# Linear attention beside a gated MLP on one core: the key-value sums come out turned, and q moves to groups of 128 and 64 columns

## The chip, the cores and the metric

The kernel runs on one core of one Trainium2 chip. A core has TensorE (matrix multiplication; it reads its operands from SBUF and writes its sums to PSUM), VectorE, ScalarE, GpSimd (POOL in the profile) and SyncE (SP, which here only issues DMAs). PSUM has eight banks of 128 partitions by 512 fp32 values. The metric is the device time of one launch in microseconds. Each kernel is run several times and the median counts. The profile comes from one further execution.

## The reference, cut to what matters

```python
xn = _layernorm(x)                                   # x: 2048 x 576
q, k, v = split(xn @ wqkv)                           # 32 heads of 18 columns
phi = lambda t: jnp.where(t > 0, t + 1, jnp.exp(t)) + 1e-6
pq, pk = phi(q), phi(k)
kv = jnp.einsum("bhsd,bhse->bhde", pk, v)            # one 18 x 18 matrix a head
z = jnp.einsum("bhsd->bhd", pk)
num = jnp.einsum("bhqd,bhde->bhqe", pq, kv)
den = jnp.einsum("bhqd,bhd->bhq", pq, z)[..., None] + 1e-6
s = (num / den).reshape(B, S, D) @ wo                # 2048 x 576
h = gelu(xn @ w_gate) * (xn @ w_up)                  # 2048 x 4608
return x + s * silu(h @ w_down)
```

There is no mask over time: kv and z are sums over all 2048 tokens, so no query can be finished before all keys and values are done.

## The kernel before, in words

Tokens are held in four blocks (tb = 0 to 3) of 512, and each block in four tiles of 128. The 576 columns of x are two halves of 288 = 128 + 128 + 32 rows of contraction. Precision is kept by splitting operands into a high and a low part in fp32r, a fast matmul type: a product is hi x hi + hi x lo + lo x hi. PASSES (line 40) lists seven such matmuls for a half of the contraction, in which the 32-row remainders share one; a product over both halves takes 14.

The program has these stages:

1. **Weights, normalization, k and v** (lines 917 to 998). w_tiles, load_w, load_w2, prep_hi and prep_lo bring the weights in and split them: ScalarE writes the high part, VectorE or POOL the low part. load_w2 loads both column halves of q for one half of the contraction into the slot b12; the second such load waits until POOL is done with the first. For each tile of tokens k_mm and v_mm make k and v, k_post applies phi, and v_post copies v into va, in groups of seven heads (126 columns; the last group has four heads, 72 columns) with a column of ones behind each group. kv_mm multiplies pk by va for each of the five groups and accumulates over all 16 tiles into two PSUM banks (kv_a, kv_b): rows are columns of k, columns are columns of v, and the column of ones gives z.
2. **q** (lines 1000 to 1023). q_mm makes one group of q for a block of 512 tokens, transposed: 14 matmuls with the weights of 126 or 72 columns as the stationary operand. Blocks 0 and 1 are stored to DRAM (q_store) and reloaded later (q_load); 2 and 3 stay in SBUF (q_hold, which can run a list of other work between its groups).
3. **kv times wo** (kv_done, kv_turn, kv_wo; lines 419 to 479). kv_done masks the sums to their heads' 18 x 18 blocks (kvm), and builds zc, which holds z by head. kv_turn transposes kvm on TensorE (kt) and ScalarE copies it to kvt. kv_wo multiplies it by wo in fp32, two matmuls a group (kw), and splits the results into kvh and kvl (kv4 for the last group). The output projection is thereby folded into the sums.
4. **den, scale, s** (lines 498 to 551), for blocks 2, 3, 0, 1 in this order. den multiplies zc by q in fp32 (d: five matmuls of 32 columns by 512 tokens), takes the reciprocal on VectorE and splits it into rd, high and low. scale spreads a head's reciprocal to its columns with the 0/1 matrix sel (b: two fp32r matmuls a group, high and low, with 32 rows), multiplies q by it and splits the product into pq. s_mm makes a tile of 128 tokens of s: 15 passes (5 groups by 3) for two column halves, 30 matmuls of 288 columns.
5. **Gated MLP**: the matrices of the gate and the up projection by a scheme of seven products for a 2 x 2 block multiplication (matrix, lines 627 to 666), then the down projection (down_all). The change does not touch this code.

In stage 1, and again from line 1063 on (`fixed[0] = True`), instructions that go through act, vec and mm keep the written order on their engines. From line 1000 to 1062 (`fixed[0] = False`) a planner orders them: each engine's queue is filled by priority in written order, and an instruction whose operands or buffers the planner expects late lets later ones pass. Once ordered, each engine works its queue strictly in order. SP issues DMAs in order, too, and holds at one that has to wait.

PSUM is given out by pools. Up to line 1015 the pool has two single banks and two pairs beside the two sum banks; `banks(4, 2)` (line 1018) opens one with four single banks and two pairs. A new pool waits until the old one has been emptied. SBUF slots named by big(i, ...) hold different tiles one after the other; b12 serves the raw q weights, then four operand copies, then wo, then sel and rd.

## Time and profile before

| what | us |
|---|---|
| median of 3 runs | 1565.93 |
| lowest and highest | 1565.88, 1567.93 |
| the profiled execution's own time | 1567.46 |
| its span | 1565.8 |
| TensorE busy | 1526.4 |
| VectorE, ScalarE, GpSimd busy | 1077.4, 550.1, 558.5 |
| first product of the gated MLP begins | 355.89 |

The profiled execution's own time includes what lies around the span. In the profile an operation's row names the line, the engine, the tile that it writes and those that it reads, and its shape: partitions by elements. A matmul's row says rows of contraction by stationary columns. PEld rows are loads of the stationary operand, which overlap with matmuls. An fp32 matmul shows as two records, an fp32r matmul as one. Matmuls are pipelined, so a record lasts longer than the distance to the next one's start. The chain of waits is followed back from the last instruction, at each step to what released it; its rows give a start, a length and a count.

### The profile page before, as it was taken

How to read it: one execution, taken by the hardware profiler on the slowest of the kernel's cores; microseconds unless marked ns; L12 is line 12 of the kernel's file. 1: busy time of each engine (PE TensorE's matmuls, PEld its weight loads, DVE VectorE, ACT ScalarE, POOL GpSimd, SP SyncE). 2: the span in 40 equal slices, each digit the busy share in tenths (PEclk: the TensorE clock that was granted, in tenths of full speed). 3: DMA queues.
4: the chain of work that ended last, by engine and by line, in shares of the span. 5: the costliest groups of instructions: out<-in, count | busy, mean ns of one | idle time of the engine just before them, and what ended most of it. 6: DMA issues, size and time to landing. Idle time of an engine off the chain costs nothing.

```text
span 1565.8 us, 22593 instructions
## 1 busy us (share of the span) xinstructions
PE 1526.4 (97%) x8569; PEld 1346.7 (86%) x8569; DVE 1077.4 (69%) x1565; ACT 550.1 (35%) x939; POOL 558.5 (36%) x513
## 2 busy tenths in 40 slices
PE   4999999999999999999999999999999999999998
PEld 4987995888888888888888888888889999999998
DVE  6668336544887787777787877778885565655775
ACT  3435214233322223222322232323234555444443
POOL 3143523022655544456555544565440020000220
PEclk9999999999999999999999999999999999999999
DMA  4326000444443433344434333344469757787873
GB/s 151 131 108 234 1 5 0 168 167 174 165 165 129 162 120 124 135 154 165 165 140 154 140 109 143 138 165 165 157 218 329 249 164 270 241 260 248 279 248 112
DMA packets 112287, 256.60 MB, mean 164 GB/s; under 512 B 10086, under 2 KB 38502, under 8 KB 110134
## 3 DMA queue, kind: packets, MB, share of 16 engines
q1 hardware_dynamic: 110114, 242.31, 43.7%
q0 software_dynamic: 2064, 12.85, 2.3%
q8 instruction: 67, 1.10, 0.3%
q14 instruction: 42, 0.34, 0.1%
HBM read 157.47 MB, written 97.65 MB: 163 GB/s over the span
## 4 chain that ended last, share of the span: by engine, by line
PE 91%; DVE 5%; ACT 2%; DMA 1%; issue 1%; POOL 0%; DVEq 0%; ACTq 0%; POOLq 0%
PE bd L827 25%; PE al L622 14%; PE ga L622 14%; PE de L622 14%; PE be L622 7%; PE s L539 4%; PE q L370 3%; PE pv L99 3%; PE pk L99 2%; PE d L501 1%; PE kv_a L99 1%; PE b L516 1%; PE xt L171 1%; DVE xo_B L96 1%; DVE x L96 1%
## 5 line engine op out<-in xcount | busy, mean ns | idle before, releaser
L827 PE MATMUL bd<-t,s 128*128 128x288 f32 x3024 | 401.5, 295 | 2.2 <-DVE u L96 2.2
L827 PEld LDWEIGHTS bd<-t,s 128*128 128x128 f32 x3024 | 400.9, 188 | 2.8 <-DVE u L96 2.7
L96 DVE TENSOR_TENSOR s<-sr,s 128x512 fp32r<-128x512 f32 x252 | 181.1, 760 | 119.7 <-ACT s L93 117.8
L93 ACT ACTIVATE s<-sr 128x512 fp32r<-128x512 f32 x252 | 149.0, 625 | 192.4 <-PE bd L827 128.4
L102 POOL TENSOR_TENSOR hs<-h,h 128x512 f32<-128x512 f32 x72 | 100.5, 1405 | 231.2 <-DVE h L96 228.4
L93 ACT ACTIVATE h<-h 128x512 f32<-128x512 f32 x108 | 67.1, 633 | 247.5 <-DVE h L96 132.1
L102 POOL TENSOR_TENSOR sx<-sx 128x288 f32<-128x288 f32 x24 | 27.9, 1183 | 318.6 <-DVE sx L96 317.6
L96 DVE TENSOR_TENSOR wa<-raw,wa 128x256 fp32r<-128x256 f32 x72 | 77.2, 1072 | 56.2 <-ACT wa L93 53.0
L102 POOL TENSOR_TENSOR sm<-raw 128x384 f32<-128x384 f32 x72 | 75.6, 1050 | 96.9 <-DMA raw<-in_wgu_dram 79.3
L96 DVE TENSOR_TENSOR h<-h,u 128x512 f32<-128x512 f32 x108 | 97.6, 904 | 3.7
L102 POOL TENSOR_TENSOR td<-td 128x288 f32<-128x288 f32 x72 | 71.5, 993 | 57.4 <-DMA td<-in_wd_dram 53.2
L93 ACT ACTIVATE wa<-sm 128x1152 fp32r<-128x1152 f32 x36 | 41.8, 1160 | 139.3 <-PE de L622 139.3
L96 DVE TENSOR_TENSOR wa<-sm,wa 128x768 fp32r<-128x768 f32 x72 | 63.7, 885 | 33.6 <-ACT wa L93 32.8
L96 DVE TENSOR_TENSOR wb<-sm,wb 128x256 fp32r<-128x256 f32 x72 | 60.8, 845 | 20.5 <-ACT wb L93 20.0
L96 DVE TENSOR_TENSOR wb<-raw,wb 128x256 fp32r<-128x256 f32 (+1 forms) x108 | 71.8, 664 | 1.7 <-ACT wb L93 0.2
L93 ACT ACTIVATE u<-al 128x512 f32<-128x512 f32 x72 | 40.9, 592 | 91.2 <-PE al L622 91.2
L370 PE MATMUL q<-xo_B,wq 128*126 128x512 f32 (+1 forms) x240 | 66.3, 407 | 0.0
L96 DVE TENSOR_TENSOR u<-u,ga 128x512 f32<-128x512 f32 x72 | 49.4, 686 | 22.7 <-PE ga L622 22.0
L622 PE MATMUL al<-xo_B,wa 128*128 128x512 f32 x252 | 63.1, 390 | 0.8 <-ACT s L546 0.8
L622 PE MATMUL ga<-xr_B,wb 128*128 128x512 f32 x252 | 63.0, 389 | 0.0
L622 PE MATMUL be<-xo_T,wa 128*128 128x512 f32 x252 | 63.0, 390 | 0.0
L622 PE MATMUL de<-xo_T,wb 128*128 128x512 f32 x252 | 63.0, 390 | 0.0
(163 smaller groups left out, 2992.3 us busy)
## 6 DMA issues: line engine op xcount, KB each, us to landing
sr<-hs SPq DMA_DIRECT2D x252, 256.0 KB
hs<-h SPq DMA_DIRECT2D x68, 512.0 KB
raw<-in_wgu_dram SPq DMA_DIRECT2D x36, 768.0 KB
hs<-hs SPq DMA_DIRECT2D x102, 256.0 KB
td<-in_wd_dram SPq DMA_DIRECT2D x18, 576.0 KB
td<-td SPq DMA_DIRECT2D x18, 576.0 KB
tr<-td SPq DMA_DIRECT2D x16, 576.0 KB
tr<-in_wd_dram SPq DMA_DIRECT2D x12, 576.0 KB
```

The lines of the kernel that those rows point to most:

```text
L93: pin(nc.scalar.activation(*args, **kw))
L96: pin(getattr(nc.vector, op)(*args, **kw))
L99: pin(nc.tensor.matmul(*args, **kw))
L102: tc.keep_in_program_order(getattr(nc.gpsimd, op)(*args))
L171: pin(nc.tensor.transpose(xts[n][:, j, c], xs[:, j, c], ident))
L370: nc.tensor.matmul(pq[0:wdt, :], w_part(0, j, wi, gi * GW, gi * GW + wdt, rows), xo[s][nm][0:rows, xi, :], start=(n == 0), stop=(n == 2 * ...
L501: nc.tensor.matmul(pd[0:H, :], at["zc"][0:wdt, gi, :], ph[tb][0:wdt, gi, :], start=(gi == 0), stop=(gi == NHG - 1),)
L516: nc.tensor.matmul(pb[0:wdt, :], at["sel"][:, gi, 0:wdt], at["rd"][:, i, :], start=(i == 0), stop=(i == 1),)
L539: nc.tensor.matmul(pss[:, c, 0:HALF], pqs[tb, gi][a][0:wdt, t * P : (t + 1) * P], kw[0:wdt, c * HALF : (c + 1) * HALF], start=(n == 0), st ...
L622: nc.tensor.matmul(o, w[0:rows, wi, :], xop[0:rows, xi, :], start=(start and n == 0), stop=(n == len(PASSES) - 1), skip_group_check=True,)
L827: nc.tensor.matmul(banks[j][:, 0:HALF], hw[n, s][:, a, t * P : (t + 1) * P], w[:, c, g % 4], start=(new and g == 0 and m == 0), stop=(g == ...
```

## The change

In kv_mm the operands swap: va is stationary and pk moves, so the sums come out as columns of v by columns of k, which is the form that kv_wo needs as its stationary operand. The ones move to the first column of va, so z is row 0 of each group. kv_turn is dropped. wo gets a zero row 0 and two more columns, of which one has a 1 in row 0: kv_wo thereby yields z as an extra column, from which zc is made.

q's groups become five of 128 columns. The last group had 72 columns; 64 of them stand twice in group 4 (rows 0 to 63 and 64 to 127), and the other eight are dealt out, two each, into rows 126 and 127 of groups 0 to 3. The host lays out the q weights so (wq, 640 columns, apart from wkv). In group 4, pq then holds the high part in rows 0 to 63 and the low part in rows 64 to 127, and kv4 holds the high part twice and, in a second tile, the low part with zeros below: two passes do what three did. The rows of kvh, kvl and zc for the eight dealt-out columns are brought to partitions 126 and 127 by twelve small DMAs on SP's queue.

den makes its block in two column halves, tokens 0 to 255 to PSUM rows 0 to 63 and tokens 256 to 511 to rows 64 to 127, each with z twice. VectorE then takes the reciprocal over 128 rows by 256 columns. rd holds high and low rows of both halves with zeros elsewhere, sel holds the 0/1 matrix four times, and scale needs one matmul of 128 rows.

In the order, kv_wo moves into the list of q_hold(2) behind the third group, ahead of the change of pools; make_sel follows; den(2) moves behind the first group of q_hold(3). The scratch of POOL-issued DMAs goes from 4096 to 2048 bytes.

```diff
 def load_w2 / prep_hi / prep_lo
-        raw = big(i, [P, 2, 3, HALF], F32, f"rw_{m}_{j}")
+        raw = big(i, [P, 2, 3, NC2[m]], F32, f"rw_{m}_{j}")
...
 def kv_mm
-                kv_out(gi)[0:wdt, 0 : wdt + 1],
-                pk[:, gi * GW : gi * GW + wdt], va[:, gi, 0 : wdt + 1],
+                kv_out(gi)[0 : wdt + 1, 0:wdt],
+                va[:, gi, 0 : wdt + 1], pk[:, gi * GW : gi * GW + wdt],
...
 def q_mm
-                    pq[0:wdt, :],
-                    w_part(0, j, wi, gi * GW, gi * GW + wdt, rows),
+                    pq, w_part(0, j, wi, gi * P, (gi + 1) * P, rows),
...
 def make_masks
+        nc.gpsimd.memset(mask[0:1, :], 1.0)
...
+        nc.gpsimd.memset(at["zc"][Q4:P], 0.0)
...
 def load_wo
+        at["wo"] = w = big(12, [P, 4, D + 2], F32, "wo_t")
+        at["wo4"] = w4 = tmp([P, D + 2], "wo4")
+        for t in (w, w4[:, None, :]):
+            nc.gpsimd.memset(t[0:1, :, 0:D], 0.0)
+            nc.gpsimd.memset(t[:, :, D:], 0.0)
+            nc.gpsimd.memset(t[0:1, :, D : D + 1], 1.0)
...
-    def kv_turn():
...
 def kv_wo
+        for gi in (4, 0, 1, 2, 3):
...
+            r, x_ = slice(0, Q4 if gi == 4 else GW), slice(Q4, W4)
+            z, src = pw[:, 1, HALF : HALF + 1], pw[:, :, 0:HALF]
+            if gi == 4:
+                nc.vector.tensor_copy(zx[x_], z[x_].to_broadcast([W4 - Q4, 2]))
+                parts(kv4[x_, 2, :], kv4[x_, 3, :], src[x_])
+                nc.scalar.activation(two(kv4[Q4:P, 0, :]), src[r], AF.Copy)
+
+            nc.vector.tensor_scalar(
+                zc[r, gi, :].rearrange("p (r h) -> p r h", r=2),
+                mh[r, gi, None, :].to_broadcast([r.stop, 2, H]), z[r], None, op0=ALU.mult,
             )
+            if gi == 4:
+                parts(kv4[r, 0, :], kv4[r, 1, :], src[r])
+            else:
+                parts(kvh[r, gi, :], kvl[r, gi, :], src[r])
+        for gi in range(4):
+            r, e = slice(Q4 + 2 * gi, Q4 + 2 * gi + 2), slice(GW, P)
+            nc.sync.dma_start(
+                out=zc[e, gi, :].rearrange("p (r h) -> p r h", r=2)[:, :, H - 1], in_=zx[r]
+            )
+            for t, i in ((kvh, 2), (kvl, 3)):
+                nc.sync.dma_start(out=t[e, gi, :].bitcast(F32), in_=kv4[r, i, :].bitcast(F32))
...
 def make_sel
+        for i in range(4):
+            r = slice(i * H, (i + 1) * H)
+            if i % 2:
+                nc.scalar.activation(sel[r], one, AF.Copy)
+            else:
+                nc.gpsimd.tensor_copy(sel[r], one)
...
 def den
+        for gi in range(NHG):
+            for i in range(2):
+                nc.tensor.matmul(
+                    pd[2 * H * i : 2 * H * (i + 1), 0:HB], at["zc"][:, gi, :],
+                    ph[tb][:, gi, i * HB : (i + 1) * HB],
+                    start=(gi == 0), stop=(gi == NHG - 1),
+                )
+        r = gl_tile([P, HB], f"r_{tb}")
...
+        for i in range(2):
+            c = slice(i * HB, (i + 1) * HB)
+            rows, low = slice(2 * H * i, 2 * H * (i + 1)), slice(H * (2 * i + 1), 2 * H * (i + 1))
+            nc.scalar.activation(rd[rows, c], r[rows], AF.Copy)
+            nc.vector.tensor_sub(rd[low, c], r[low], rd[low, c].bitcast(F32))
 def scale
-        for i in range(2):
-            nc.tensor.matmul(
-                pb[0:wdt, :], at["sel"][:, gi, 0:wdt], at["rd"][:, i, :],
-                start=(i == 0), stop=(i == 1),
-            )
+        nc.tensor.matmul(pb, at["sel"][:, gi, :], at["rd"], start=True, stop=True)
...
 def s_mm
+        steps = [
+            (pqs[tb, gi][a], kw[:, gi, :])
+            for gi in range(4) for a, kw in ((0, at["kvh"]), (0, at["kvl"]), (1, at["kvh"]))
+        ] + [(pqs[tb, 4][0], at["kv4"][:, i, :]) for i in range(2)]
...
-    q_hold(2, 7, [kv_done, kv_turn])
+    q_hold(2, 7, [kv_done, lambda: None, kv_wo])
+    make_sel()
     psum["stage"].close()
     stage.close()
     banks(4, 2)
-    kv_wo()
-    make_sel()
-    den(2)
     differences(1, nc.gpsimd)
-    q_hold(3, 8, [lambda: None, lambda: None, lambda: scale(2, 0),
+    q_hold(3, 8, [lambda: den(2), lambda: None, lambda: scale(2, 0),
                   lambda: (scale(2, 1), scale(2, 2)), lambda: (scale(2, 3), scale(2, 4))])
...
-        "TRN2", target_bir_lowering=False, num_devices=1, dynamic_dma_scratch_size=4096
+        "TRN2", target_bir_lowering=False, num_devices=1, dynamic_dma_scratch_size=2048
```

More of the change, by code (lines that the diff above doesn't have):

```diff
@@ L32 @@
 W4 = WIDTHS[4]
+Q4 = 64
+Q2 = NHG * P // 2
 LN_EPS = 1e-5
@@ new lines, in make_sel @@
+    def make_sel():
+        n = NHG * P
+        buf = big(12, [P, n + TBN], F32R, "aux")
+        at["sel"] = sel = buf[:, 0:n].rearrange("p (g j) -> p g j", g=NHG)
+        at["rd"] = rd = buf[:, n : n + TBN]
+        one = tmp([H, NHG, P], "self")
+        nc.gpsimd.memset(one, 1.0)
+        four, last = one[:, 0:4, 0:GW], one[:, 4, :].rearrange("p (r j) -> p r j", r=2)
+        for o, pattern, base in ((four, [[GW, 4], [1, GW]], 0), (last, [[0, 2], [1, Q4]], 4 * GW)):
+            nc.gpsimd.affine_select(
+                out=o, in_=o, compare_op=ALU.is_ge, fill=0.0, base=base,
+                pattern=pattern, channel_multiplier=-DH,
+            )
+            nc.gpsimd.affine_select(
+                out=o, in_=o, compare_op=ALU.is_ge, fill=0.0, base=DH - 1 - base,
+                pattern=[[-s_, n_] for s_, n_ in pattern], channel_multiplier=DH,
+            )
@@ L530, in s_mm @@
+        h = slot([P, 2, TBN], F32R, f"pq_{tb}_{gi}")
+        pqs[tb, gi] = [h[:, i, :] for i in range(2)]
+        split(h[:, 0, :], h[:, 1, :], p)
     def s_mm(tb, t):
```

200 lines of the change are left out of this document (86 added, 114 removed).

## The prediction

> **What bounds the kernel now.** I read the page first, then the chain of waits from 215 us to 360 us, because the diff touches work only up to there; the gated matrices and the down projection behind it (355.89 us to the end) keep their code.
>
> ```profile
> PE 1526.4 (97%) x8569; PEld 1346.7 (86%) x8569; DVE 1077.4 (69%) x1565; ACT 550.1 (35%) x939; POOL 558.5 (36%) x513
> PE 91%; DVE 5%; ACT 2%; DMA 1%; issue 1%; POOL 0%; DVEq 0%; ACTq 0%; POOLq 0%
> ```
>
> TensorE is busy 97% of the span and makes 91% of the chain that ended last. A TensorE instruction that goes away is therefore worth its issue spacing, unless another engine then ends the wait. The same chain by time, in the stage that the change rewrites:
>
> ```profile
> by line: PE s L539 45.7%; PE q L370 19.8%; PE d L501 12.4%; PE b L516 7.3%; PE kw L469 3.7%; PE pv L99 2.6%; PE al L622 2.4%; PE pk L99 1.7%; PE kv_a L99 1.2%; issue 1.2%; PE kt L451 0.5%; PE be L622 0.5%; ACT s L546 0.5%; ACT kvt L455 0.4%
> 225.15 0.45 PE kt L451 x4
> ...
> 226.32 0.26 PE kt L451
> ...
> 236.61 1.48 issue
> 238.09 2.18 PE kw L469 x8
> ...
> 311.94 2.51 PE b L516 x10
> 314.45 4.41 PE d L501 x10
> 318.87 16.12 PE s L539 x120
> 334.99 2.63 PE b L516 x10
> 337.62 17.50 PE s L539 x120
> ...
> 355.89 3.48 PE al L622 x14
> ```
>
> Columns are start, length, what, and how many instructions. The four token blocks run in the order 2, 3, 0, 1; the rows from 311.94 are the full period of block 0 (23.05 us to 334.99) and then block 1, which has no den behind it. Within a period TensorE goes from b to d to s with no gap. Of the 145 us, s has 45.7%, d 12.4% (18.0 us, 4.5 a block), b 7.3% (10.6 us).
>
> **The change, part by part.** *s, 14 passes for 15.* Each of 16 s_mm calls issues 28 matmuls of 288 columns where it issued 30. A full block takes 16.12 us for 120, so 0.134 us each; 32 go: -4.30 us. The columns copied into spare rows ride in matmuls that run anyway.
>
> *b, one spread matmul for two.* 40 become 20, at 2.51/10 = 0.25 us: 10.6 us becomes 5.3. The contraction grows from 32 to 128 rows, at the same 512 columns. Not all of the 5.3 is kept, because b also covers VectorE:
>
> ```profile
> 312.63 1.88 DVE L527 TENSOR_TENSOR ph<-ph,b 126x512 f32<-126x512 f32 x3 [10.01 <-PE b L516]
> 314.43 1.89 DVE L109 TENSOR_TENSOR pq<-ph,pq 126x512 fp32r<-126x512 f32 x3
> 319.62 3.34 DVE L507 RECIPROCAL r<-r 32x512 f32<-32x512 f32 x1
> 335.68 1.88 DVE L527 TENSOR_TENSOR ph<-ph,b 126x512 f32<-126x512 f32 x3 [8.05 <-PE b L516]
> 340.73 1.29 DVE L109 TENSOR_TENSOR pq<-ph,pq 126x512 fp32r<-126x512 f32 x2 [0.17 <-ACT pq L108]
> ```
>
> A multiply takes 0.63 us and frees one of the four single banks; five b in 1.25 us outrun it. The fifth b waits for the first multiply and den for the second, so den begins near 0.35 + 2 x 0.63 = 1.6 us instead of 1.25: 0.4 us goes back in blocks 3 and 0. VectorE needs from 335.68 to 342.02 (6.3 us) for block 1's multiplies and subtractions. s consumes a group each 0.8 us and can take the next tile's matmuls meanwhile, so I return 0.6 us in block 1. Net -3.9 us (ends -5.3 and -2.5).
>
> *Clock in block 1.* s takes 17.50 us there against 16.12 in block 0, with the same 120 matmuls.
>
> ```profile
> 336.00:339.00 3.00, 3.00 (x13) 2.23 (x12) 3.00 (x6) 1.84 (x3) 0.00 (x0) 0.71 0.81 262
> ```
>
> That is a stretch of 3 us: after its length come the busy times of the engines, and the third number from the end is the granted clock. It is 0.71, right behind 2.63 us of b on 32 rows. With half as many b, on 128 rows, I expect no dip: -1.4 us (ends -1.4 and 0).
>
> *kv_turn goes.* The sums come out turned, so five transposes and two copies leave the chain: 225.15 to 226.60, 1.45 us including the wait for ScalarE. Swapping operands in kv_mm keeps 80 fp32 matmuls, one column narrower: nothing.
>
> *den in halves.* Ten fp32 matmuls of 256 columns stand where five of 512 stood, the halves to PSUM rows 0-63 and 64-127.
>
> ```profile
> L501 PE MATMUL d<-ph,small x40: 589/592/617, 240.2 to 318.3; 126*32 126x512 f32 x32, 72*32 72x512 f32 x8
> ```
>
> One fp32 matmul shows as two records of 0.592 us, begun 0.441 us apart. In series the halves cost the same 4.4 us, and no gain is one end. The two halves share neither array columns nor PSUM rows, and if each pair runs side by side the block costs 2.2 us; with a start-up of 0.15 (0.592 - 0.441) I say 2.4. Over four blocks: -8.0 us (ends -8.8 and 0). No row shows two matmuls with disjoint columns. The nearest is that TensorE begins a record before its predecessor ends and loads weights under it (86% beside 97%), so it overlaps what shares nothing; I take the side-by-side end. VectorE's reciprocal drops from 3.34 to about 1.7 us (half the columns, four times the rows), which gives slack but is hidden. Two ScalarE copies and two subtractions for one each also fit, since s covers them.
>
> A weighing on den: the row says that d ends at 314.45 + 4.41 = 318.86 and s begins at 318.87, so leaving a 32-column matmul costs nothing visible. The Trainium skill ("TensorEngine Tiling (Array Packing)", section Key Properties) says that changing the tiling mode drains TensorE. By that rule eight edges at the 0.151 us by which records overlap would give back 1.2 us, and the sum would be 1549.8 for 1548.6 below; by the row it is nothing, and this case's trace speaks against it for this edge.
>
> *kv_wo earlier, with small transfers.* It moves from after the change of PSUM pools (236.61, the 1.48 us wait for the last q to be evacuated) to behind the third q group of block 2. Its ten matmuls (290 columns for 288) stay. Their waits for ScalarE and VectorE, filled by d before, are now filled by the fourth and fifth q.
>
> ```profile
> L108 ACT ACTIVATE kvh<-kw x4: 650/650/651, 239.3 to 243.4; 126x576 fp32r<-126x576 f32 x4
> L109 DVE TENSOR_TENSOR kvl<-kw,kvh x4: 757/757/758, 240.0 to 244.1; 126x576 fp32r<-126x576 f32 x4
> 1.26 0.90 SPq L248 DMA_DIRECT2D rw<-in_wqkv_dram  x2
> 0.81 2.98 DMA x<-in_xe_dram
> 236.26 0.61 POOL L487 MEMSET self<- 32x630 f32 x1
> ```
>
> Group 4 has three ScalarE copies and two subtractions, 3 x 0.65 + 0.76 = 2.7 us before its bank is free; 6.6 us of q lie beside that. The pool change still waits for the last q: 1.48 us as before. Twelve transfers then queue on SP at 0.45 us each (two issued in 0.90), and each lands at most 2.98 us after its issue (the row of a load of 384 KB). den(2), now behind the first q group of block 3, needs the first ten of them (the fourth den column is tenth): 4.5 + 2.98 = 7.5 us after group 4 is cut. Until then TensorE has two q groups (6.6), the other four kw (4.4), the pool change (1.48) and a q group (3.3), 15.8 us, less the 2.7 of the cut: 13 us of cover. If it is gone, den(2) holds TensorE. SP's next behind them is the reload of stored q, which waits for scale(2) anyway. POOL's selector work grows to some 4.4 us (one memset and two copies of that size, five selects of that size or smaller, two short memsets) and can hold back the last q addition that den(2) reads: +1.0 us (ends 0 and +3). The memsets ahead of the wo loads, and those in the masks, queue on POOL among its additions; POOL is busy 36% of the span, so 0. The POOL-issued reloads get half the descriptor space:
>
> ```profile
> xr_T<-kept_T POOLq DMA_DIRECT2D x4, 1280.0 KB, 8.6
> ```
>
> Each lands in 8.6 us, and the last two are issued behind scale(1) with four tiles of s (about 15 us) and two products (2 x 3.17) ahead of their first reader: 0, unless they queue.
>
> *Prep of the q weights.* 320 columns for 288, on a stretch of chain not set by TensorE:
>
> ```profile
> 87.83 0.82 ACT wq L93
> 88.71 0.81 POOL wq L272
> 89.53 2.29 POOL wq_l L272
> 91.89 0.80 POOL wq L272
> 92.72 4.41 DMA rw<-in_wqkv_dram
> 97.15 0.93 ACT wq L93
> ...
> 106.56 1.61 PE kv_a L99 x6
> ```
>
> The six steps sum to 10.06 us and 11% of that is 1.1 us. The 2.29 is a POOL operation held up by VectorE and a transfer has a fixed part, so I take +0.7 us (ends +0.4 and +1.1). q itself stays 14 matmuls a group:
>
> ```profile
> 127.48 3.28 PE q L370 x14
> 362.54 3.17 PE ga L622 x14
> ```
>
> q with 126 weight columns takes 3.28, a gate product with 128 takes 3.17. If 128 columns are the reason, 20 groups give 2.2 us. Both stream 512 columns 14 times, so I take the difference for something at a group's edge, and count 0 (ends -2.2 and 0). Phi, stores and reloads of 128 rows for 126 take the same free sizes: 0.
>
> The sum: -4.3 - 3.9 - 1.4 - 1.45 - 8.0 + 1.0 + 0.7 = -17.35 us. The profiled execution took 1567.46 us with a span of 1565.8; the median of the three runs is 1565.93, so the span stands for the median, and the forecast is **1548.6 us**. Ends taken together: 1540 to 1564.
>
> **The rivals.** *The halves run one after the other.* Then den keeps 4.4 us a block: 1548.6 + 8.0 = 1556.6 us. For it: every matmul in this trace begins only when its predecessor has streamed, and den's record pairs too. Against it: only that they share nothing. The Trainium skill ("TensorE: Matmul & The Clock Gate", Part 3) states that matmuls on separate column groups run at once, 2.38 times faster for three of 32 columns; no run here shows it yet, and that rule is for my forecast.
>
> *The planner's new order loses cover.* From 108 us on the engine orders come from a planner that fills waits; with den and b halved, s of block 2 may wait for VectorE's multiplies and subtractions (0.63 us each, ten a block, beside its builds of the token differences' operands), and b of block 3 for its reciprocal. Half of den's saving, 4 us, and 2 us more go: 1554.6 us.
>
> *Slower: the small transfers.* If each completes before SP begins the next, the ten take 10 x (0.45 + 2.98) = 34.3 us; 13 are covered, and den(2) holds TensorE, with all later q queued behind it in order, for 21.3: 1565.93 - 17.35 + 21.3 = 1569.9 us. It decides above (13 + 17.35)/10 = 3.0 us a transfer. Against it: SP issued two loads in 0.90 us while the first transfer was still on its way (0.81 to 3.79).
>
> **How the numbers follow.** Side by side, near 1548.6 (1544 to 1552): 0.45. In series, 1556.6 (1553 to 1560): 0.25. Lost cover, 1554.6 (up to 1562): 0.13. The slower rival and other stalls of that size: 0.13. Between, within 0.2% (3.1 us, about what a measurement can tell): 0.04. Faster thus 0.83, same 0.04, slower 0.13. The range takes the first three: 1544 to 1562 us.
>
> **What would show it.** s: 112 matmuls a block in 15.05 us. b: five in about 1.25 to 1.6 us. d: 2.4 us for ten steps if side by side, 4.4 if not. No kt rows; clock 1.00 throughout block 1; the first q behind 106.56 + 0.7 us. A TensorE gap in front of den(2) released by a transfer, or gaps ahead of s released by VectorE beyond a microsecond each, would make the prediction wrong, as would a den in series.

## The result, and the profile after

The changed kernel takes **1550.65 us** (median of four executions, 1549.25 to 1552.65) where the kernel before takes 1566.93 on the same chip (1565.88 to 1567.93): a ratio of 0.9894, 95% interval 0.9882 to 0.9905, so 1.06% faster. The forecast was 1548.6 us, with 1544 to 1562 as its range. The profiled execution took 1550.36 us with a span of 1548.7, so the span shrank by 17.1 us; the first product of the gates, which the prediction took as the end of the changed stage, begins at 338.46 instead of 355.89 us, 17.43 us earlier. Nearly all of the gain is in that stage.

The page of the changed kernel, busy times and the shares of the chain that ended last:

```profile
PE 1507.1 (97%) x8552; PEld 1343.1 (87%) x8552; DVE 1075.0 (69%) x1571; ACT 553.6 (36%) x945; POOL 563.8 (36%) x512
PE 90%; DVE 6%; ACT 2%; DMA 1%; issue 1%; POOL 0%; SPq 0%; ACTq 0%; DVEq 0%; POOLq 0%
```

TensorE lost 19.3 us of busy time (1526.4 to 1507.1); the other engines moved by at most 5.3 us. It is still the bound, but VectorE's share of the chain rose from 5% to 6%; its new waits in the changed stage stand in the next view. It is the chain of waits of the changed kernel in the same stage; columns are start, length, what, count:

```profile
243.78 3.45 PE q L374 x14
247.23 2.31 PE d L546 x20
...
301.44 0.25 PE b L565
301.71 0.70 DVE ph L567
302.48 0.64 ACT pq L112
303.16 0.40 PE s L588
303.56 2.31 PE d L546 x20
305.87 14.99 PE s L588 x111
320.86 0.25 PE b L565
...
322.59 15.10 PE s L588 x112
...
338.46 3.47 PE al L669 x14
```

Read it against the rows of before. den takes 2.31 us where it took 4.41. The ten b of 2.51 us have become one b of 0.25 in the chain and a new wait: VectorE multiplies (0.70), ScalarE rounds (0.64), and only then has s its first operand. The timeline of TensorE at that border (start, length from the first record's start to the last one's end, operation; in brackets the idle time ahead and what ended it) shows what TensorE does meanwhile:

```profile
301.27 1.67 PE L565 MATMUL b<-aux 128*128 128x512 f32 x5
303.16 0.40 PE L588 MATMUL s<-kvh,pq 128*128 128x288 f32 x1 [0.21 <-ACT pq L112]
```

All five b run inside the wait, and TensorE is idle for only 0.21 us of it. From the first b to the first s it is 1.89 us; five b without a wait take 1.15 (half of the ten in 2.29 us that a run below shows), so the wait costs some 0.74 us a border. s takes 112 matmuls in 15.4 us (0.40 + 14.99) where it took 120 in 16.12. The period of block 0, from its b to block 1's b, is 320.86 - 301.44 = 19.42 us; it was 23.05. Block 1 takes 338.46 - 320.86 = 17.60 us; it was 20.90 (334.99 to 355.89).

For sums over the stage I take, in each kernel, the time from the first q behind the last kv_b to the first product of the gates. That is 132.64 us before (223.25 to 355.89) and 113.27 after (225.19 to 338.46): 19.37 us less. The stage begins 1.94 us later than before, so the chain ahead of it lost that; and behind it 0.33 us more went (17.43 at the first product, 17.1 at the end).

### The profile page after: what moved, and what is told of

Same layout as the page of the kernel before. It is cut to its first block, busy times and chain, and to the rows that moved or that the text cites. A ratio compares the mean times of both kernels' runs of the same rounds, so it can differ in the third digit from the quotient of the medians.

```text
span 1548.7 us, 22597 instructions
## 1 busy us (share of the span) xinstructions
PE 1507.1 (97%) x8552; PEld 1343.1 (87%) x8552; DVE 1075.0 (69%) x1571; ACT 553.6 (36%) x945; POOL 563.8 (36%) x512
## 4 chain that ended last, share of the span: by engine, by line
PE 90%; DVE 6%; ACT 2%; DMA 1%; issue 1%; POOL 0%; SPq 0%; ACTq 0%; DVEq 0%; POOLq 0%
PE bd L874 25%; PE al L669 15%; PE de L669 15%; PE ga L669 15%; PE be L669 7%; PE s L588 4%; PE q L374 3%; PE pv L103 2%; PE pk L103 2%; PE kv_a L103 1%; DVE xo_B L100 1%; PE xt L176 1%; PE d L546 1%; DVE x L100 1%; DVE bn L100 1%
## 5 line engine op out<-in xcount | busy, mean ns | idle before, releaser
L374 PE MATMUL q<-xo_B,wq 128*128 128x512 f32 x240 | 66.7, 404 | 1.6 <-ACT e_q L97 1.5
L669 PE MATMUL al<-xr_B,wa 128*128 128x512 f32 x252 | 63.0, 389 | 0.0
L669 PE MATMUL be<-xr_T,wa 128*128 128x512 f32 x252 | 63.0, 389 | 0.0
```

What stands on the lines that cost most here:

```text
L374: nc.tensor.matmul(pq, w_part(0, j, wi, gi * P, (gi + 1) * P, rows), xo[s][nm][0:rows, xi, :], start=(n == 0), stop=(n == 2 * len(PASSES) ...
L669: nc.tensor.matmul(o, w[0:rows, wi, :], xop[0:rows, xi, :], start=(start and n == 0), stop=(n == len(PASSES) - 1), skip_group_check=True,)
```

## The experiments

Kernels called "changed" below are the changed kernel with one edit, and "before" the kernel before with one edit. Each time stands beside runs of the unchanged kernel before on its own chip. "The stage" is the stretch just defined, in the one execution that was profiled. The changed kernel was profiled twice, with 113.27 and 113.49 us, so a difference of a few tenths between two stages says nothing.

### den's halves one behind the other

```diff
 def den
-        for gi in range(NHG):
-            for i in range(2):
+        for i in range(2):
+            for gi in range(NHG):
```

The same ten matmuls, on the same rows and columns; only their order on TensorE differs.

> The changed kernel with one edit: den runs all five groups of the first column half, then all five of the second, instead of alternating. Same matmuls, same operands, same result. Theory (the halves run side by side because neighbours in the queue use different array columns): the pairs are no longer neighbours except at the one boundary, so den goes from 2.31 us a block to about 4.2 to 4.4 us, and the kernel gets 7.5 to 8.5 us slower than the changed one (near 1558 to 1559 us). Rival (the gain comes from the form, 64 columns by 256, and not from running at once): den stays at 2.3 us a block and the time at 1550.5 us.

Measured: 1557.92 us against 1568.11, ratio 0.9932 (0.9918 to 0.9947). The stage takes 118.87 us, 5.60 more than the changed kernel's. Its chain, and the same matmuls by time:

```profile
308.75 3.65 PE d L546 x20
312.40 14.98 PE s L588 x111
```

den takes 3.65 us for the 2.31 of the changed kernel. With the pair of halves next to each other in the queue, twenty records take 0.115 us each; with five of one half first, 0.18 each. So the order alone gives 1.34 us a block, and the halves of the changed kernel do run side by side: their pairs of records begin 0.007 us apart. The theory's size was 7.5 to 8.5 us, though, and 5.6 came: halves queued one behind the other still overlap a little, at the seam. In the trace the records of one half begin 0.215 us apart (twenty in series would take 4.3 us), and the first record of the second half begins at 310.03 us, while three of the first half's are still to begin (310.24, 310.45, 310.67). The four dens account for 4 x 1.34 = 5.4 of the 5.6 us. That the halves cost the same in any order (the rival, 0) fell.

### den's halves alone, in the kernel before

```diff
 def den
-            nc.tensor.matmul(pd[0:H, :], at["zc"][0:wdt, gi, :], ph[tb][0:wdt, gi, :], ...)
+            for i in range(2):
+                nc.tensor.matmul(
+                    pd[2 * H * i : 2 * H * i + H, 0:hb], at["zc"][0:wdt, gi, :],
+                    ph[tb][0:wdt, gi, i * hb : (i + 1) * hb], ...)
-        nc.vector.tensor_scalar(r, pd[0:H, :], EPS, None, op0=ALU.add)
+        for i in range(2):
+            nc.vector.tensor_scalar(r[:, i * hb : (i + 1) * hb],
+                pd[2 * H * i : 2 * H * i + H, 0:hb], EPS, None, op0=ALU.add)
```

> The kernel before with one edit: den in two column halves of 256 tokens, 32 stationary columns each, the first to PSUM rows 0 to 31, the second to rows 64 to 95; the reciprocal and all else as before (two small VectorE copies for one). Theory: the halves run side by side, den goes from 4.41 to about 2.3 us a block, and the time falls by 7.5 to 8.5 us against the kernel before, because b alone covers most of the wait for VectorE. Rival 1 (in series with 32 columns): 0. Rival 2 (den was the cover of VectorE's multiplies and subtractions in the kernel before, so the wait comes up behind it): about half, 4 us.

Measured: 1560.94 us against 1568.11, ratio 0.9949 (0.9933 to 0.9966). The stage takes 125.44 us, 7.20 less than before's 132.64. The chain of this kernel:

```profile
310.68 2.28 PE d L503 x20
312.97 16.12 PE s L546 x120
329.09 2.52 PE b L523 x10
```

With 32 stationary columns instead of 64, den again takes 2.28 us for twenty records: 4.41 - 2.28 = 2.13 a block. Everything else in the period stands as before, ten b of 2.52 and 120 s of 16.12. The times agree (7.17 us less). So both rivals fell, in series (0) and half of it taken back by a wait (4 us), and this is the largest single part of the change, done alone.

### s with its fifteenth pass put back

```diff
 def s_mm
-        ] + [(pqs[tb, 4][0], at["kv4"][:, i, :]) for i in range(2)]
+        ] + [(pqs[tb, 4][0], at["kv4"][:, i, :]) for i in (0, 1, 1)]
```

The low part of group 4 counts twice in this kernel, so its output differs in the last digits.

> The changed kernel with one edit: s takes a 15th pass (group 4's second pass is issued twice, so the low part of that group's weights counts twice and the result differs slightly from the reference). Theory (a pass of s is on TensorE's path and costs its issue spacing): 32 more matmuls of 288 columns at 0.134 us, +4.3 us against the changed kernel. Rival (s has slack behind VectorE's wait): under +2 us.

Measured: 1554.60 us against 1568.10, ratio 0.9914 (0.9899 to 0.9928); the stage takes 117.74 us, 4.47 more than without the pass. In its chain:

```profile
308.79 16.05 PE s L588 x119
```

119 matmuls in 16.05 us are 0.135 each; the 32 that the change takes away are worth 4.3 us by that row and 4.47 by the stage. The term of the prediction holds, and s has no slack (the rival).

### The spread matmul twice

```diff
 def scale
-        nc.tensor.matmul(pb, at["sel"][:, gi, :], at["rd"], start=True, stop=True)
+        for _ in range(2):
+            nc.tensor.matmul(pb, at["sel"][:, gi, :], at["rd"], start=True, stop=True)
```

> The changed kernel with one edit: scale issues its spread matmul twice, the second writing the same values over the first, so that b has its old count of 40. Theory (part of b was cover for VectorE and ScalarE, which now end the wait ahead of s): of 20 x 0.226 = 4.5 us about 1.3 us is hidden, +3.2 us against the changed kernel (1553.5 us). Rival 1 (b counts in full): +4.5 to 5 us. Rival 2 (b is hidden wholly behind VectorE): under +1 us. On the clock: if the length of b brings the half clock behind block 1, it shows again there (s of block 1 near 16.5 us instead of 15.1); if 32 rows or the chance position of a window did, s stays at 15.1 us.

Measured: 1552.86 us against 1568.11, ratio 0.9899 (0.9885 to 0.9914); by the times alone it can't be told from the changed kernel. The stage takes 115.55 us, 2.28 more than the changed kernel's. The chain of block 3:

```profile
284.31 2.29 PE b L566 x10
286.60 2.31 PE d L546 x20
288.91 14.86 PE s L589 x112
```

Here b is ten matmuls again, 2.29 us, and d follows without a wait. VectorE's and ScalarE's 1.4 us, which stand in the chain of the changed kernel, lie beside b and d. So most of what the five saved matmuls would bring in a block (1.15 us) is taken back by that wait: blocks 3 and 0 come out at 19.46 and 19.71 us against 19.37 and 19.42. Block 1, without den to cover, gains 0.44 (18.04 to 17.60), and the rest, about 1.4 us, is in block 2, where scale stands between the q groups. I had expected 3.2 us. And there is no half clock behind block 1's b in this kernel either, so ten spread matmuls on 128 rows do not bring the dip.

### The spread over 128 rows, in the kernel before

```diff
 def make_sel
-        at["sel"] = sel = buf[0:H, 0:n].rearrange("p (g j) -> p g j", g=NHG)
-        at["rd"] = buf[0:H, n : n + 2 * TBN].rearrange("p (i t) -> p i t", i=2)
-        one = tmp([H, NHG, GW], "self")
+        at["sel"] = sel = buf[:, 0:n].rearrange("p (g j) -> p g j", g=NHG)
+        at["rd"] = buf[:, n : n + 2 * TBN].rearrange("p (i t) -> p i t", i=2)
+        nc.gpsimd.memset(at["rd"].bitcast(F32), 0.0)
+        one = tmp([P, NHG, GW], "self")
...
```

Still two matmuls a group, but over 128 rows, 96 of them zero: more rows and nothing else.

> The kernel before with one edit: the two spread matmuls read 128 rows instead of 32, the other 96 rows of both operands being zeros. Same count of matmuls, same result. Theory (32 rows by themselves cost: 0.251 us a matmul against 0.226 with 128, slower q matmuls around them, and the half clock behind block 1's b): 40 x 0.025 = 1.0, some 0.6 at the borders with q, 1.4 of clock, together -2 to -3.5 us against the kernel before, s of block 1 at 16.1 us instead of 17.5. Rival (rows do not matter and the half clock falls by chance): within 1 us of the kernel before, b at 2.5 us a block.

Measured: 1564.75 us against 1568.10, ratio 0.9980 (0.9970 to 0.9989); the stage takes 129.67 us, 2.97 less than before. The chain of this kernel, first at block 2 and then at block 1; and the rows of before that stand at the first place:

```profile
258.85 0.47 PE b L517 x2
259.32 3.27 PE q L370 x14
...
334.65 2.34 PE b L517 x10
336.98 15.95 PE s L540 x120
```

```profile
258.06 0.65 PE b L516 x2
258.72 3.46 PE q L370 x14
```

Ninety-six rows of zeros make the kernel faster. A pair of b takes 0.47 instead of 0.65 us, the q group behind it 3.27 instead of 3.46, ten b 2.34 (block 0: 2.32) instead of 2.63 (2.51). Block 1's s takes 15.95 us instead of 17.50, with the clock at 1.00 all through. So two things that the prediction put down to fewer matmuls come with the rows alone: the dip of the clock goes (1.55 us), and about 1.4 us more at the ends of each stretch of b. It is the ends and not the matmuls themselves: within a stretch, b begin 0.23 us apart with 32 rows as with 128, and my 0.251 for 0.226 was an average over the ends. Ahead of block 1, from the last s to the first b it is 0.22 us with 32 rows and 0.14 with 128, and from there to the second b 0.34 and 0.24.

The clock, in a window of 3 us: the third number from the end is the granted clock, the first after the length is TensorE's busy time. The changed kernel behind block 1's b:

```profile
321.00:324.00 3.00, 2.71 (x15) 1.91 (x14) 2.87 (x5) 2.44 (x4) 0.00 (x0) 1.00 0.51 166
```

It is 1.00 there, where before had 0.71 with TensorE 3.00 of 3.00 us busy. Over all profiled executions of this study, the half clock behind block 1's b stands in three of three whose b has 32 rows (the kernel before, den's halves alone, and the run after this one), and in none of the nine whose b has 128 rows. A TensorE that shows as busy with 32-row matmuls for 2.5 us was thus followed by the lower clock that elsewhere in these traces follows a gap. The Trainium skill ("TensorE: Matmul & The Clock Gate", Part 1) has the clock follow how busy TensorE has been; these rows agree only if busy time in the profile isn't what is counted.

The dip does not follow every such stretch, and place matters too. In every trace a half clock lasts 3.41 us or twice that (but for the one in which the execution ends), and within one execution these stretches begin whole multiples of 3.41 us apart (in the changed kernel at 33.12, 50.18, 104.80 and 156.00 us, which is 5, 16 and 15 such steps). This is the one of the kernel before, behind block 1's b:

```profile
337.25:340.66 3.41, 3.41 (x15) 3.11 (x14) 3.31 (x6) 1.63 (x4) 0.00 (x0) 0.50 0.71 237
```

There are nine stretches of ten b on 32 rows in blocks 3, 0 and 1. Five of them put at least 2.33 us into one step, and in four of these half clock fills the next step (block 1 in each of the three kernels; block 3 in the run after this one). The other four put at most 2.04 us into one step, and none follows. On 128 rows, three stretches of ten b put 2.25 to 2.33 us into one step (block 0 here, blocks 0 and 1 with the spread twice), and none follows. So in comparable places it is the rows that go with the dip. Block 1 of this very run is no test, since a border of two steps cuts its b; its ten executions speak for it, with 3.35 us less between the medians.

### q with 128 weight columns, in the kernel before

```diff
 def q_mm
+        wide = P if gi < 4 else wdt
-                    pq[0:wdt, :], w_part(0, j, wi, gi * GW, gi * GW + wdt, rows),
+                    pq[0:wide, :], w_part(0, j, wi, gi * GW, gi * GW + wide, rows),
```

> The kernel before with one edit: q's groups 0 to 3 load 128 weight columns instead of 126 (the next two columns of the same tile, whose two rows of the result nobody reads). Theory (the width of the stationary operand sets the spacing of q's matmuls): a q group of 14 goes from 3.28 us to 3.17 us, 16 groups save 1.8 us against the kernel before; the four groups of 72 columns keep 3.28. Rival (the width does nothing, and the quicker q of the changed kernel has another reason, such as the new weight layout): 3.28 us stays and so does the time.

Measured: 1567.46 us (ten executions) against 1568.11 (thirteen), ratio 0.9996 (0.9987 to 1.0006). One group, in the chain of this kernel:

```profile
126.81 3.25 PE q L371 x14
```

3.25 us for 14 matmuls against 3.28 with 126 columns: the width does next to nothing, and my theory (1.8 us) fell. (The stage of this one execution is 1.63 us longer than before's, for the second half clock, in block 3, that the section before this one counts.) The prediction's zero was right. Its reason, something at a group's edge, wasn't tried at this place; next to b, the run before this one moved a q group from 3.46 to 3.27 us by the rows of its neighbour alone.

### kv_wo at its old place

```diff
-    q_hold(2, 7, [kv_done, lambda: None, kv_wo])
-    make_sel()
+    q_hold(2, 7, [kv_done])
     psum["stage"].close()
     stage.close()
     banks(4, 2)
+    kv_wo()
+    make_sel()
```

> The changed kernel with one edit: kv_wo and make_sel go back behind the change of PSUM pools, as in the kernel before; den(2) stays behind the first q group of block 3. Theory (either place has other matmuls to fill kv_wo's waits for ScalarE and VectorE, so the move itself is worth little, and the small transfers are covered in either): 0 to +2 us against the changed kernel. Rival (the early place is what keeps TensorE fed while the sums are split and the small transfers land): +3 us or more, as gaps ahead of kw or of den(2).

Measured: 1552.06 us against 1568.10, ratio 0.9896 (0.9879 to 0.9912); the stage takes 113.75 us, 0.48 more than the changed kernel's. Its chain around kv_wo:

```profile
238.59 2.14 PE kw L479 x8
240.73 2.97 PE q L374 x13
243.70 2.19 PE kw L479 x8
246.11 1.01 PE d L546 x6
```

Behind the pool change, the order of the planner again puts q of block 3 and pieces of den(2) into kv_wo's waits. The move is worth half a microsecond at most, which two executions can't tell from nothing (against the second one of the changed kernel it is 0.26). The theory (0 to +2 us) held, and the rival (+3 or more) fell. In the changed kernel SP issues the small transfers like this (queue rows: start, length, line, how many):

```profile
231.62 1.54 SPq L500 DMA_DIRECT2D small<-eps_t  x2
...
239.58 0.56 SPq L504 DMA_DIRECT2D kvl<-kv  x1
```

Two take 1.54 us of the queue and a single one 0.56, more than the 0.45 that I took from the loads; the twelve are issued from 231.62 to 240.14 us. den(2) begins at 247.23, directly behind q (243.78 + 3.45 = 247.23), so it waits for none of them.

### The spread ahead of the previous block's last tile

```diff
-    def scale(tb, gi):
+    def spread(tb, gi):            # matmul and VectorE's multiply
...
+    def cut_q(tb, gi):             # the split of ph into high and low
...
         for t in range(TT):
+            if t == TT - 1 and tb in den_next:
+                for gi in range(NHG):
+                    spread(den_next[tb], gi)
             s_mm(tb, t)
...
```

Block 2's loop has the same for block 3, and ahead of each block only cut_q is left. The wait at each border (0.70 VectorE, 0.64 ScalarE) suggested this: do the spread and the multiply one row tile of s earlier, so that s never waits for them.

> The changed kernel with one edit: the spread matmuls and VectorE's multiplies of the next block (3, 0 and 1) are issued ahead of the fourth tile of s of the block before; only the splitting into high and low stays behind it. Theory (in those blocks TensorE waits for spread, multiply and copy one after the other; 1.13 + 2.31 + 15.0 = 18.4 us of matmuls stand against periods of 19.4): the wait goes, 0.9 us in blocks 3 and 0 and 0.7 us in block 1, -2.5 us against the changed kernel. Rival (the wait is for the slots of the split operands, which are free only when that tile of s is done): no change.

Measured: 1549.82 us against 1568.10, ratio 0.9883 (0.9868 to 0.9898). The stage takes 111.43 us, 1.84 less than the changed kernel's. The chain at block 0's border, and TensorE's timeline at block 3's:

```profile
296.60 0.93 PE b L565 x4
297.53 0.26 PE s L595 x2
```

```profile
278.75 0.69 PE L595 MATMUL s<-kvh,pq 128*128 128x288 f32 x4
279.58 1.20 PE L565 MATMUL b<-aux 128*128 128x512 f32 x4
```

At 296.60, b and s follow each other without a wait. Ahead of block 3 the chain leaves TensorE at 277.59 us and runs through ScalarE and VectorE, which have the reciprocals of den(3) split only at 279.54. I took these 2.0 us for a gap of TensorE, and so tried it without block 3. The timeline says otherwise: TensorE goes on with s of block 2 until 279.44, and is idle for 0.14 us.

### The same for blocks 0 and 1 only, and the changed kernel once more

```diff
         for gi in range(NHG):
-            cut_q(tb, gi)
+            scale(tb, gi) if tb == 3 else cut_q(tb, gi)
...
```

The edit is shown against the kernel of the section before; block 3's early spread in block 2's loop goes, too.

> Like the run with the early spread, but only for blocks 0 and 1: their spread stands ahead of the last row tile of s of the block before, and block 3 has spread and cut together behind s of block 2 as in the changed kernel. Theory (at a block's border TensorE waits for the chain of VectorE and ScalarE that makes the first group of normed q; an early spread hides it only where the reciprocals are long done): the 2.0 us gap ahead of block 3 goes, the borders of blocks 0 and 1 stay without a wait, the stage from the first q to the first product of the gates is some 1.5 to 2 us shorter than with all three early, about 109.5 to 110 us against 111.43, and the time is 2 to 4 us below the changed kernel, ratio of the time before 0.9865 to 0.9885. Rival (the gap ahead of block 3 only moves, since rd of block 3 comes late wherever the spread stands): the stage stays at 111 to 111.5 us and the time within 1 us of the run with all early.

> The changed kernel once more, on the same chip, for a direct comparison with the early spread of two blocks and for a second profiled execution. Theory (the half clock at 156 to 162 us of its first profiled execution falls there by the place of a 1.5 us gap of TensorE and isn't fixed by the change): this execution may lack it, and its first product of the gates would then start some 1.7 us earlier, near 336.7 us; the time stays at 1549 to 1552 us. Rival (the change's later q weights set the dip): it stands at 156 to 162 us again.

Measured, all on one chip: 1550.91 us (ratio 0.9879, 0.9859 to 0.9899) with the early spread, 1551.04 (0.9888, 0.9873 to 0.9903) for the changed kernel, against 1568.35. The two can't be told apart, and no version was found that is measurably faster than the changed kernel. In the traces the stage takes 111.85 us with two early spreads and 113.49 in this second execution of the changed kernel. The chain with the early spread, at block 0's border:

```profile
299.20 0.93 PE b L565 x4
300.13 0.26 PE s L595 x2
300.39 0.32 PE b L565
300.72 3.46 PE s L595 x26
```

The theory (1.5 to 2 us below the run with all three) fell: there was no gap of TensorE to remove. Ahead of block 3 the chain of VectorE and ScalarE stands again as in the changed kernel, and the stage is 0.42 us longer than with all three. The rival's idea, a gap that only moves, falls with it, though its numbers (111 to 111.5 us) come close.

Why an early spread brings so little can be read here. It takes VectorE's and ScalarE's 1.34 us out of the chain and puts four b more into it that had run inside the wait. What is left is less than a microsecond a border: from den to den it is 18.54 us (285.64 to 304.18) against 19.41 (284.15 to 303.56) in the changed kernel.

In the stage that still makes 1.64 us for two borders, and the times show none of it. In the profiled executions the clock accounts for that. The early spread's comes to the stage 0.88 us later (226.69 for 225.81), and it has half clock far behind the stage, where neither execution of the changed kernel has any. The view of the clock shows it, first with the early spread and then in the second execution of the changed kernel:

```profile
1144.00:1147.00 3.00, 3.00 (x15) 3.00 (x15) 3.00 (x2) 0.63 (x1) 2.92 (x4) 0.54 0.17 63
```

```profile
1144.00:1147.00 3.00, 2.45 (x18) 2.45 (x19) 2.96 (x3) 0.63 (x1) 2.92 (x3) 1.00 0.37 104
```

The half clock lasts 3.41 us and costs half of that, 1.7. So whether the early spread pays is open: the stage says some 1.6 us, and four executions a kernel can't tell.

The second execution of the changed kernel also answers where the 1.94 us ahead of the stage come from. First the rows of the q weights' preparation in the changed kernel:

```profile
87.55 0.90 ACT wq L97
88.53 0.88 POOL wq L278
89.40 2.36 POOL wq_l L278
91.83 0.87 POOL wq L278
92.73 5.11 DMA rw<-in_wq_dram
97.86 1.01 ACT wq L97
...
107.18 2.04 PE kv_a L103 x8
```

The six steps sum to 11.13 us for 10.06, and kv_a begins 0.62 us later, as forecast (0.7). But by 126 us only 0.13 of that is left: TensorE runs at half clock here until 111.63 us (111.97 before), and the later start loses 0.48 us less to it. The rest of the 1.94 is another stretch at half clock, in windows of the changed kernel's first and second execution:

```profile
156.00:159.00 3.00, 3.00 (x16) 2.90 (x15) 1.67 (x6) 1.39 (x4) 0.00 (x0) 0.50 0.00 0
159.00:162.00 3.00, 3.00 (x17) 2.51 (x16) 1.30 (x4) 1.27 (x4) 0.00 (x0) 0.93 0.00 0
```

```profile
156.00:159.00 3.00, 2.85 (x17) 2.88 (x17) 2.22 (x6) 1.38 (x5) 0.00 (x0) 0.61 0.03 12
159.00:162.00 3.00, 3.00 (x15) 2.48 (x15) 1.42 (x4) 1.75 (x4) 0.00 (x0) 0.82 0.00 0
```

3 x 0.50 + 3 x 0.07 = 1.7 us go in the first, 3 x 0.39 + 3 x 0.18 = 1.7 in the second. I had taken this dip for the luck of one execution, and it stands again at the same place, so the theory fell; with the 0.13 it makes up the 1.94. It is in five of the eight profiled executions of the changed kernel and its variants, and in none of the four of the kernel before and its variants. Ahead of it TensorE has two gaps, one on each side of a group of transposes. The first is 0.95 to 1.02 us in those eight and 0.57 to 0.77 in the four, the second 0.71 in all. What decides is where the gaps fall in the steps of 3.41 us. In the five, both lie in one step, which so holds 1.69 to 1.73 us of idle time, and half clock fills the next step. In the other three a border of two steps cuts the first gap, and no step holds more than 1.40 us. In the four without the change it is at most 1.47, also where both gaps lie in one step. So the change makes a gap long enough for a half clock to follow, and the place of the steps, which differs from execution to execution, decides whether it does. Two of the three executions without it (the spread twice, kv_wo at its old place) come to the stage no earlier, at 225.97 and 225.92, since another stretch at half clock, from 33 us on, lasts 6.83 us in them and 3.41 in the changed kernel. The first q of the stage begins at 224.4 to 226.7 us in the eight and at 222.2 to 224.6 in the four: the part ahead of the stage costs about 2 us on average, with a scatter of a microsecond either way.

Each such dip costs about 1.7 us. The Trainium skill ("TensorE: Matmul & The Clock Gate", Part 1) states that activity is counted in free-running windows of some 3.4 us and that the phase varies from run to run. The steps of 3.41 us in these traces agree, and so does their place: a step begins 0.33 us ahead of the first of the two gaps in the changed kernel, and 3.10 us ahead of it with the spread twice. The dip near 1144 us fits as well. All twelve executions have two gaps there, 0.51 to 0.87 and some 1.71 us. A half clock follows in four, in which one step holds 1.72 to 2.24 us of idle time. It does not in seven with at most 1.56, nor in one with 1.71 (the run with the fifteenth pass).

## Why the prediction was right

The forecast was 2.05 us too low against the median (1548.6 for 1550.65), and right by its mechanism; two of its reasons were wrong, and two misses nearly cancel. The ends that it gives, 1540 to 1564, are not what its terms add up to: these come to 1542.9 and 1561.8. By its own steps:

**den side by side, -8.0.** Measured -7.2 alone on the kernel before. A block takes 2.28 to 2.31 us; 2.4 was forecast, 4.4 if in series. Confirmed, and the run with the halves apart shows that it is the order in TensorE's queue that does it. It also bears out the rule cited from the Trainium skill ("TensorE: Matmul & The Clock Gate", Part 3) with the number 4.41 / 2.31 = 1.9 for two halves. The rival "in series" (1556.6) is out; the kernel with the halves apart, with 3.65 us a block still not wholly in series, lost 5.6 us of the gain.

**s, -4.3.** Measured -4.47 (-4.25 against the second execution of the changed kernel). Confirmed.

**b, -3.9, and the clock in block 1, -1.4.** Together -5.3, and the two runs give 2.28 (the count) + 2.97 (the rows) = 5.25. The sum holds; its division doesn't. I gave the count nearly all, less 0.4 and 0.6 for VectorE's multiplies. What failed is the working of that cover: I had den held until the second multiply, with s then fed. In the trace the first s waits for the first multiply and ScalarE's rounding at the borders of the last three blocks, and den comes behind that s. So the count brought only 2.3 us, and the step "half as many b" was worth 0.1 to 0.4 us in each of the last three blocks. In its place came what I had put at nothing: a stretch of 32-row matmuls costs about 0.2 us at each end beside 128-row ones. The clock's term was right in place and size (1.55 for 1.4). Of its two reasons the 128 rows are shown to be enough; half as many b may be enough too, as 32-row stretches with at most 2.04 us in one step had no dip, but no run has five b on 32 rows. That the kernel before had its dip behind block 1 in the profiled execution is in part luck, since it hangs on where the steps fall.

**kv_turn, -1.45.** Not tried alone. The parts that were measured, 7.20 + 4.47 + 2.28 + 2.97 + 0.48, make 17.40 of the 19.37 us; kv_turn's 1.45 would bring them to 18.85. Half a microsecond stays unassigned, and a whole one if kv_wo's 0.48 is nothing; five differences of two executions each can't tell more.

**kv_wo and the small transfers, +1.0 (0 to +3).** None of it came: the new place gained 0.48 us at most, den(2) waits for no transfer, POOL held nothing back. The slower rival fell with it: it needed more than 3.0 us a transfer, and the twelve took 8.5 us of SP's queue in all, with den(2) 7.1 us behind.

**The q weights, +0.7.** The step was 0.62 at kv_a, then hidden down to 0.13. In its place stand 1.7 us of half clock at 156 us, which no step of the prediction had: this term of the sum was too small by 1.2 (1.94 for 0.7). The stage itself gave 19.37 us for the 18.05 of its terms, 1.3 more, mostly the kv_wo term (-0.48 or nothing for +1.0). The two misses nearly cancel: with the 0.33 us behind the stage, the span shrank by 17.1 for the forecast 17.35. Between the medians it is 16.3 us (1566.93 to 1550.65), 1.07 short of the forecast, and the kernel before stood 1.0 us higher in these runs than the 1565.93 that the forecast set out from; these two make the 2.05.

**q with 128 columns, 0.** Confirmed by a run of its own.

**The drain, 0 by the row, 1.2 by the rule.** The row was misread. In the chain a piece always ends where the next begins, so d's end at 318.86 and s's begin at 318.87 can't show a cost. The begins of single matmuls in the trace can. In the kernel before, the first s begins 0.52 us behind the last d, where d stand 0.43 apart, and the second s 0.24 behind the first, where s stand 0.13 apart: leaving den costs some 0.2 us. It does so in the changed kernel too (0.31 for 0.21, and 0.24 for 0.13), so that this hardly moves the sum. For b the edges are what the change removes: a border between 32-row and 128-row matmuls costs about 0.2 us on each side (0.65 to 0.47 and 3.46 to 3.27). The Trainium skill's rule ("TensorEngine Tiling (Array Packing)", section Key Properties), that a change of tiling mode drains TensorE, agrees with all of these; I had weighed it against a row that could not show it, and left out b's edges.

**The planner loses cover, 1554.6.** The wait for VectorE and ScalarE at three borders is this rival's, at 0.74 us each, 2.2 for its 6. Block 2's s did not wait.

## What to carry to other kernels

Two small matmuls on disjoint columns of TensorE ran side by side as neighbours in its queue, and with one half queued behind the other only at the seam; so write the loop over the halves inside the loop over the accumulation. When a stage loses matmuls, look for what they covered: here half of b's matmuls were cover for VectorE and ScalarE, and taking that wait away in turn exposed the matmuls that had run inside it. Look at the engine's timeline before you call a stretch of the chain a gap of it, and at single begins before you call an edge free. And for a matmul with few rows, look at its neighbours and at the granted clock behind it before you count it as cheap: filling its rows with zeros can pay.

## What the runs showed of the hardware

- Zero rows made a kernel faster: two spread matmuls over 128 rows instead of 32, same count, gave 2.97 us in the stage and a ratio of 0.9980 (0.9970 to 0.9989).
- A TensorE that the profile shows as 100% busy, with 32-row matmuls, was followed by a half clock (0.71 in the kernel before, with 3.00 of 3.00 us busy), in four of five cases with at least 2.33 us of them in one step of 3.41 us. With 128-row matmuls it never was, in nine executions, also in three cases with 2.25 to 2.33 us of them in one step.
- Half clock came in steps: it lasts 3.41 us or twice that (but for the last one of an execution), and begins whole multiples of 3.41 us apart within an execution. At the two places looked at in all twelve executions, a step with 1.69 us or more of TensorE idle was followed by half clock in nine of ten cases, and none of the others, with at most 1.56.
- Leaving an fp32 matmul of 32 or 64 stationary columns for a full one cost some 0.2 us in the begins of the matmuls, though the chain shows no wait there.
- Halves queued one behind the other still overlap at the seam: 3.65 us for twenty records that stand 0.215 us apart within a half, with the second half's first record beginning ahead of three of the first half's.
- A transfer of at most 4.5 KB on SP's queue took 0.56 to 0.77 us to issue, where two loads of weights took 0.90 together.
